# Transposing K as fp32 pairs and multiplying V two rows at a time in a decode attention kernel

## The chip, the cores and the metric

The kernel runs on one core of one Trainium2 chip. The metric is device time in microseconds (us) of that core. Every number below is from fast runs. The queue that issues DMA transfers is SP's; PE is the TensorE matmul engine, PEld its weight loads (counted apart, they overlap PE: busy 1139 and 817 us in a span of 1375 in before), DVE the VectorE, ACT the ScalarE, POOL the GpSimd. "GB/s" is what the core's 16 DMA engines moved.

## The reference, cut to what matters

```
x (1,1,448); k_cache, v_cache (1, 8, 65536, 256) bf16; 16 query heads, 2 per K/V head
q = x @ wq                                   # 16 heads of 256
s = q . k / sqrt(256);  p = softmax(s);  o = p . v
a = o @ wo
b = (relu-gated FFN of a second x: 448 -> 1792 -> 448)
g = sigmoid(sum(x * gate_w));  out = g * a + (1 - g) * b
```

K and V are 268 MB each and every byte is used once. The arithmetic per byte is small (PE is busy 1139 and DVE 1006 of 1375 us in before), so the limit taken here is the time in which 549 MB (with the weights) can be read: 1286 us at the 427 GB/s of the stretch where only V arrives.

## The kernel before

The K rows of a head come in 16 groups of 4096 rows (2 MB), 32 rows to a partition. A group goes one of two ways. A **T group** goes to PE: transpose K, evict by ACT, multiply by q (QK). A **D group** goes to DVE, which multiplies and sums each row with a broadcast q. The constant `ND_PER_HEAD` says how many of the 16 are D groups: 6 and 5 in turn. A V group goes to PE (PV). The loads go into three rings of 2 MB slots: three for T, two for D, three for V.

```python
def emit_tp(slot, blk, c, bank):              # T: 8 rows x one half of the head dim
    kb = KTp[bank][:].bitcast(BF16)
    for jj in range(8):
        j = blk * 8 + jj
        transpose(out=kb[:, jj*128:(jj+1)*128], in_=tring[:, slot, j, c*128:(c+1)*128], identity=ident)

def emit_qk(g, sl0, kbufs, sphys, ...):       # 2 slots x 2 halves, 512 columns each
    for sp_ in range(2):
        for c in range(2):
            matmul(S_ps[sphys], lhsT=zq[:, g, c, 63-r:191-r], rhs=kts[:, kbufs[c], sp_*512:(sp_+1)*512])

def emit_pv(g, grp, slot, j0, j1, ...):       # one row of V for each matmul
    for j in range(j0, j1):
        matmul(O_ps[qd:qd+2, 0:256], lhsT=lhs, rhs=vring[:, slot, j, :])
...
```

All loads are issued from one in-order queue, SP's. Their order is fixed when the program is built: a small scheduler in the builder keeps estimated costs (`D_TP`, `D_QK`, `D_V`, ...) and picks at each moment the load whose engine will run dry first. On the chip, SP waits for the slot of the next load in that order, even if another ring has a free slot: by the author's count from the trace of after, about 24 us of its loss fell where SP waited for a T slot while a V slot stood free. The FFN weights are loaded at the end into the memory of the K ring.

```python
cands.append((pri, c, g, grp, slot))     # for c in "TDV", if its next slot is free
...
cands.sort()                             # the least work ahead of its engine goes first; T before V
...
dma_q.append((..., emit_wdma(key, dst, src, ring_keys_for(e0, e1)), ..., k_all_consumed))   # FFN weights
```

## Time and profile before

The time before is 1374.0 us (median of 15 runs, 1369.6 to 1379.5).

| | before |
|---|---|
| bytes read | 549 MB |
| rate while only V arrives (1300 to 1320 us) | 424 GB/s; 424 to 429 in the windows around it |
| PE, DVE, ACT busy | 1139, 1006, 413 us |
| T group on PE | 7.03 us |
| D group on DVE | 22.1 us (64 products, 346 ns apart) |
| one 2 MB transfer at 427 GB/s | 4.9 us |

The head of the page of before, busy time and share of the span, with the DMA queues (packets, MB, share of 16 engines' span):

```profile
span 1375.1 us, 30278 instructions
...
PE 1138.9 (83%) x11218; PEld 816.5 (59%) x11218; DVE 1006.4 (73%) x5706; ACT 413.0 (30%) x834; POOL 12.9 (1%) x29
...
q1 hardware_dynamic: 45186, 549.05, 96.2%
q8 instruction: 87, 1.43, 0.4%
q14 instruction: 62, 0.51, 0.1%
```

Data alone hold the 16 DMA engines 96% of the span, and no compute engine is near that.

Windows of 20 us of before: the stretch, its length, then busy us of PE, PEld, DVE, ACT and POOL with their instructions in brackets, then granted PE clock, DMA share, GB/s:

```profile
0.00:20.00 20.00, 1.46 (x22) 1.35 (x23) 0.00 (x0) 0.00 (x0) 5.43 (x12) 1.00 0.82 269
200.00:220.00 20.00, 20.00 (x210) 14.33 (x208) 12.45 (x67) 8.21 (x16) 0.00 (x0) 0.97 0.71 286
540.00:560.00 20.00, 20.00 (x235) 14.80 (x234) 20.00 (x117) 12.02 (x23) 0.00 (x0) 1.00 0.90 366
1160.00:1180.00 20.00, 7.96 (x112) 7.05 (x112) 0.42 (x3) 0.00 (x0) 0.00 (x0) 0.59 0.70 248
1300.00:1320.00 20.00, 15.06 (x134) 10.86 (x133) 0.00 (x0) 0.00 (x0) 0.00 (x0) 1.00 1.00 424
```

The last line is the undisturbed stream. The others show where it falls short: the start, stretches in which PE is busy all the time, and the FFN weights. At 427 GB/s, 549 MB take 1286 us, so 1374 - 1286 = 88 us are lost somewhere.

The chain of waits of before, in a stretch of T groups alone (start us, us, what):

```profile
97.34 1.79 PE KTp L427 x32
99.13 0.86 PE S_ps L441 x4
99.99 0.45 PE KTp L427 x8
100.44 0.86 PE S_ps L441 x4
101.30 1.34 PE KTp L427 x24
102.64 1.73 PE S_ps L441 x8
```

From one block of 32 transposes to the next (97.34 to 104.37) 7.03 us pass: 64 transposes at 56 ns and 16 QK matmuls at 216 ns.

What the SP queue of before waited for (us in total, times, longest):

```profile
SPq L137 <- PE O_ps L571: 521.6, 93, 20.7
SPq L137 <- PE KTp L427: 472.3, 59, 31.4
SPq L137 <- DVE S_T L458: 210.9, 31, 18.7
```

SP nearly always waits for a slot, as a loader that is faster than its rings must. Most of this waiting cost nothing: these waits sum to 1205 us, the loss to 88.

### The profile page before, as it was taken

To read this page: it belongs to the slowest core of one execution; us is meant where nothing else is said; L and a number is where in the kernel's file an instruction comes from. 1 tells how busy PE (TensorE), PEld (TensorE's weight loads), DVE (VectorE), ACT (ScalarE), POOL (GpSimd) and SP (SyncE) were. 2 spreads that over 40 slices of the span, in tenths; PEclk is the share of its full clock that TensorE was granted. 3 is DMA by queue.
4 is the path that set the end of the run, shared out by engine and by line. 5 is a ranking of instruction groups with operands and counts; after the bars stand their busy time and mean duration, and the time that the engine had idled before them with its cause. 6 is when DMAs were issued, how large, how long until landed. Compare 5 with 4: busy or idle time off the path is not lost.

```text
span 1375.1 us, 30278 instructions
## 1 busy us (share of the span) xinstructions
PE 1138.9 (83%) x11218; PEld 816.5 (59%) x11218; DVE 1006.4 (73%) x5706; ACT 413.0 (30%) x834; POOL 12.9 (1%) x29
## 2 busy tenths in 40 slices
PE   4899989896899767996779897898778987687776
PEld 3577657674666545764457565576556755455554
DVE  1999997989997999799998972799939993000000
ACT  1466535440344202730026410463014620010000
POOL 1000000000000000000000000000000000000000
PEclk9999999998899978998899999999999999799999
DMA  8999998999999999999998999999999997999996
GB/s 335 397 406 413 422 426 347 413 394 430 383 405 403 417 393 377 410 426 404 420 430 352 417 398 428 410 426 413 419 419 400 417 389 317 372 427 428 426 428 292
DMA packets 45335, 550.98 MB, mean 401 GB/s; under 512 B 5185, under 2 KB 11074, under 8 KB 11970
## 3 DMA queue, kind: packets, MB, share of 16 engines
q1 hardware_dynamic: 45186, 549.05, 96.2%
q8 instruction: 87, 1.43, 0.4%
q14 instruction: 62, 0.51, 0.1%
HBM read 549.03 MB, written 0.00 MB: 399 GB/s over the span
## 4 chain that ended last, share of the span: by engine, by line
DMA 38%; PE 35%; DVE 24%; ACT 1%; issue 1%; SPq 1%; ACTq 0%; DVEq 0%
DMA vraw<-in_A_v_cache_dram 26%; DVE junk L458 23%; PE KTp L427 12%; PE O_ps L571 11%; PE S_ps L441 11%; DMA kring<-in_A_k_cache_dram 10%; DMA kring<-in_B_W_gate_dram 1%; DMA vraw<-in_A_wq_dram 1%; PE M_ps L385 1%; DMA kring<-in_B_W_up_dram 1%; DVE S_T L458 1%; ACT P_sb L503 1%; ACT kts L432 0%; SPq L371 0%; DVE MXW L472 0%
## 5 line engine op out<-in xcount | busy, mean ns | idle before, releaser
L458 DVE CUSTOM_DVE_ANT_0 junk<-kring,qb 128x256 bf16<-128x256 bf16 x2816 | 976.1, 421 | 1.4 <-DMA kring<-in_A_k_cache_dram 0.8
L432 ACT COPY kts<-KTp 128x512 f32<-128x512 f32 x672 | 355.9, 595 | 412.6 <-PE KTp L427 412.3
L571 PE MATMUL O_ps<-vraw,PT_sb 128*2 128x256 bf16 x2688 | 324.6, 282 | 101.9 <-DMA vraw<-in_A_v_cache_dram 101.4
L427 PEld LDWEIGHTS KTp<-ident,kring 128*128 128x128 bf16 x5376 | 330.1, 100 | 100.5 <-DMA kring<-in_A_k_cache_dram 39.5
L427 PE MATMUL KTp<-ident,kring 128*128 128x128 bf16 x5376 | 353.9, 223 | 35.3 <-DMA kring<-in_A_k_cache_dram 34.4
L571 PEld LDWEIGHTS O_ps<-vraw,PT_sb 128*2 128x2 bf16 x2688 | 229.4, 88 | 194.9 <-DMA vraw<-in_A_v_cache_dram 119.1
L441 PE MATMUL S_ps<-kts,zq 128*128 128x512 bf16 x1344 | 336.2, 382 | 1.1 <-ACT kts L432 1.1
L458 DVE DVE_READ_ACCUMULATOR2_ANT S_T<- 128x1 f32 x2816 | 235.3, 84 | 0.0
L571 PE MATMUL O_ps<-vraw,PTd 128*2 128x256 bf16 x1408 | 173.4, 285 | 62.4 <-DMA vraw<-in_A_v_cache_dram 62.4
L571 PEld LDWEIGHTS O_ps<-vraw,PTd 128*2 128x2 bf16 x1408 | 120.2, 87 | 114.8 <-DMA vraw<-in_A_v_cache_dram 72.3
L441 PEld LDWEIGHTS S_ps<-kts,zq 128*128 128x128 bf16 x1344 | 121.0, 98 | 103.1 <-ACT kts L432 15.9
L578 ACT COPY o_raw<-O_ps 2x256 f32<-2x256 f32 x8 | 2.9, 363 | 426.6 <-PE O_ps L571 426.6
L643 DVE SCALAR_TENSOR_TENSOR res_bf<-A_ps,gsc,res 1x448 bf16<-1x448 f32 x1 | 0.7, 671 | 154.2 <-PE A_ps L609 154.2
L543 DVE TENSOR_REDUCE den<-den 128x2 f32<-128x6 f32 x8 | 1.3, 159 | 100.7 <-POOL den L536 100.7
L472 DVE TENSOR_REDUCE MXW<-S_sb 64x1 f32<-64x512 f32 (+2 forms) x32 | 21.7, 677 | 40.6 <-ACT S_sb L448 40.1
L385 PE MATMUL M_ps<-xT,vraw 128*128 128x1 bf16 (+1 forms) x128 | 9.2, 174 | 18.5 <-DMA vraw<-in_A_wq_dram 18.5
L503 ACT ACTIVATE P_sb<-S_sb,nbias 64x512 bf16<-64x512 f32 (+2 forms) x32 | 23.0, 718 | 0.6
L496 ACT ACTIVATE nbias<-negm 128x2 f32<-128x2 f32 x8 | 1.7, 209 | 69.3 <-DVE negm L494 69.2
L400 DVE CAST zq<-M_ps 128x32 bf16<-128x32 f32 x1 | 0.3, 297 | 28.0 <-PE M_ps L392 28.0
L385 PEld LDWEIGHTS M_ps<-xT,vraw 128*128 128x128 bf16 (+1 forms) x128 | 8.3, 106 | 19.4 <-issue 18.5
L625 DVE TENSOR_SCALAR g_bf<-M_ps 128x14 bf16<-128x14 f32 x1 | 0.2, 173 | 22.2 <-PE M_ps L619 22.2
L619 PE MATMUL M_ps<-xT,kring 128*128 128x1 bf16 x112 | 8.0, 173 | 8.0 <-DMA kring<-in_B_W_up_dram 4.9
(47 smaller groups left out, 102.1 us busy)
## 6 DMA issues: line engine op xcount, KB each, us to landing
kring<-in_A_k_cache_dram SPq DMA_DIRECT2D x128, 2048.0 KB, 12.2
vraw<-in_A_v_cache_dram SPq DMA_DIRECT2D x128, 2048.0 KB, 11.6
wo_sb<-in_A_wo_dram SPq DMA_DIRECT2D x1, 3584.0 KB, 46.6
vraw<-in_A_wq_dram SPq DMA_DIRECT2D x1, 3072.0 KB, 13.3
kring<-in_B_W_down_dram SPq DMA_DIRECT2D x1, 1568.0 KB, 8.2
kring<-in_B_W_gate_dram SPq DMA_DIRECT2D x1, 1344.0 KB, 13.7
kring<-in_B_W_up_dram SPq DMA_DIRECT2D x1, 1344.0 KB, 5.6
vraw<-in_A_wq_dram SPq DMA_DIRECT2D x1, 512.0 KB, 14.8
```

Of the source, the lines that this page charges most:

```text
L385: A("pe", (lambda hc=hc, kt=kt, kk=kk: lambda e: e.matmul(M_ps[:, MC_Q + hc:MC_Q + hc + 1], lhsT=wq_sb[0:kk, kt, hc * 128:(hc + 1) * 128], ...
L427: A("pe", (lambda j=j, jj=jj: lambda e: e.transpose(out=kb[:, jj * 128:(jj + 1) * 128], in_=tring[:, slot, j, c * 128:(c + 1) * 128], iden ...
L432: A("act", lambda e: e.copy(out=kts[:, kbuf, :].bitcast(F32), in_=KTp[bank][:, :]), pr=PQ(B_K + bank), w=[("kts", kbuf)], tag=f"ev b{bank} ...
L441: A("pe", (lambda r=r, c=c, sp_=sp_, first=first, last=last: lambda e: e.matmul(S_ps[sphys][:, :], lhsT=zq[:, g, c, 63 - r:191 - r], rhs=k ...
L458: A("dve", (lambda j=j, hh=hh, col=col, ji=ji: lambda e: e.tensor_tensor_reduce(out=junk[:, ji, :], in0=dring[:, slot, j, :], in1=qb[:, g, ...
L472: A("dve", (lambda hh=hh, p0=p0: lambda e: e.tensor_reduce(out=MXW[p0:p0 + ns, pb, 2 + 2 * b + hh:3 + 2 * b + hh], in_=S_sb[p0:p0 + ns, pb ...
L496: A("act", lambda e: e.activation(out=nbias[:, pb, :], in_=negm[:, pb, :], func=ACT.Copy, scale=SCALE), r=[("negm", pb)], w=[("nbias", pb) ...
L503: A("act", lambda e: e.activation(out=P_sb[p0:p0 + ns, pb, b, :], in_=S_sb[p0:p0 + ns, pb, b, :], func=ACT.Exp, bias=nbias[p0:p0 + ns, pb, ...
L543: A("dve", lambda e: e.tensor_reduce(out=den[:, pb, :], in_=src, axis=AX.X, op=AluOpType.add), r=[("den6", pb)], w=[("den", pb)], tag=f"de ...
L571: A("pe", (lambda lhs=lhs, j=j, f_=f_, l_=l_: lambda e: e.matmul(O_ps[qd:qd + 2, 0:DH], lhsT=lhs, rhs=vring[:, slot, j, :], start=f_, stop ...
L578: A("act", lambda e: e.copy(out=o_raw[qd:qd + 2, :], in_=O_ps[qd:qd + 2, 0:DH]), pr=PQ(B_O, qd, qd + 2), w=[("oraw", pb)], tag=f"oc g{g}")
L619: A("pe", (lambda ft=ft, kt=kt, kk=kk: lambda e: e.matmul(M_ps[:, col0 + ft:col0 + ft + 1], lhsT=w_sb[0:kk, kt, ft * 128:(ft + 1) * 128], ...
```

## The change

Two bf16 neighbours are taken as one fp32, so that one transpose moves a whole row of 256 values per partition: 32 transposes in a T group instead of 64. After it, even and odd elements lie interleaved, so QK reads its moving operand with stride 2, and q is prepared in the same order. PV takes two rows at once: 4 weight columns (2 rows x 2 heads) against 512 columns of V; half of the products are not wanted and are not used. Head sums then come from two places, which doubles the small matmuls at the end of a head. `ND_PER_HEAD` becomes (6, 6): four T groups become D groups. The intent is less PE work and half the PE instructions.

```diff
-    ND_PER_HEAD=(6, 5),
+    ND_PER_HEAD=(6, 6),
...
-        def emit_tp(slot, blk, c, bank):
-            kb = KTp[bank][:].bitcast(BF16)
-            for jj in range(8):
-                    out=kb[:, jj * 128:(jj + 1) * 128], in_=tring[:, slot, j, c * 128:(c + 1) * 128], identity=ident[:]))(),
+        def emit_tp(slot, blk, bank):
+            for jj in range(4):
+                    out=KTp[bank][:, jj * 128:(jj + 1) * 128], in_=tring[:, slot, j, :].bitcast(F32), identity=identf[:]))(),
...
+            for par in range(2):
+                rhs = kts[:, kbuf, :].rearrange("p (n e) -> p e n", e=2)[:, par, :]
...
-                    O_ps[qd:qd + 2, 0:DH], lhsT=lhs, rhs=vring[:, slot, j, :], start=f_, stop=l_))(),
+                rhs = vring[:, slot, j:j + 2, :].rearrange("p a d -> p (a d)")
+                    O_ps[qd:qd + 4, 0:2 * DH], lhsT=lhs, rhs=rhs, start=f_, stop=l_))(),
...
-        D_TP, D_QK, D_EV = 0.46, 0.88, 0.52
-        D_V = J * 0.11
+        D_TP, D_QK, D_EV = 0.45, 0.46, 0.60
+        D_V = (J // 2) * 0.225
```

Cut: the same regrouping in the builder's scheduler, the q projection, and the tail of each head.

More of the change, by code (lines that the diff above doesn't have):

```diff
@@ L219, in bass_gated_mix__gqa_block_cached__glu_gated_reglu__decode_kernel @@
     GROWS = 128 * J
-    assert SK % GROWS == 0 and J % 8 == 0
+    assert SK % GROWS == 0 and J % 4 == 0
     NG = SK // GROWS
-    NBLK = J // 8
-    SLOTS_PER_GROUP = 2 * NBLK
+    NBLK = J // 4
+    SLOTS_PER_GROUP = NBLK
     ndc = CFG["ND_PER_HEAD"]
@@ L307, in bass_gated_mix__gqa_block_cached__glu_gated_reglu__decode_kernel @@
         rden = sb("rden", [128, HKV, 2], F32)
-        o_raw = sb("o_raw", [64, DH], F32)
-        oT = sb("oT", [128, 2, 4], BF16)
-        res = sb("res", [1, D], F32)
+        o_raw = sb("o_raw", [64, 2 * DH], F32)
+        oT = sb("oT", [128, 2, 8], BF16)
+        res = junk[0:1, :, :].rearrange("p a d -> p (a d)").bitcast(F32)[:, 0:D]
         res_bf = sb("res_bf", [1, D], BF16)
@@ L382, in emit_qproj @@
             for hc in range(NHC):
+                h_, e_ = divmod(hc, 2)
                 for kt in range(KT):
                     kk = ksz[kt]
-                    A("pe", (lambda hc=hc, kt=kt, kk=kk: lambda e: e.matmul(
-                        M_ps[:, MC_Q + hc:MC_Q + hc + 1], lhsT=wq_sb[0:kk, kt, hc * 128:(hc + 1) * 128],
+                    wv = wq_sb[0:kk, kt, h_ * DH:(h_ + 1) * DH].rearrange("p (n e) -> p e n", e=2)[:, e_, :]
+                    A("pe", (lambda hc=hc, kt=kt, kk=kk, wv=wv: lambda e: e.matmul(
+                        M_ps[:, MC_Q + hc:MC_Q + hc + 1], lhsT=wv,
                         rhs=xT[0:kk, kt:kt + 1], start=(kt == 0), stop=(kt == KT - 1)))(),
@@ L419, in emit_qb_ev @@
         def emit_qb_ev(g, bank):
-            A("act", lambda e: e.activation(out=qb[:, g, :, :].rearrange("p h d -> p (h d)"), in_=KTp[bank][:, :], func=ACT.Copy),
+            dst = qb[:, g, :, :].rearrange("p h (n e) -> p h e n", e=2)
+            src = KTp[bank][:, :].rearrange("p (h e n) -> p h e n", h=2, e=2)
+            A("act", lambda e: e.activation(out=dst, in_=src, func=ACT.Copy),
               pr=PQ(B_K + bank), w=[("qb", g)], tag=f"qbev{g}")
-        def emit_tp(slot, blk, c, bank):
-            kb = KTp[bank][:].bitcast(BF16)
-            for jj in range(8):
-                j = blk * 8 + jj
+        def emit_tp(slot, blk, bank):
+            for jj in range(4):
+                j = blk * 4 + jj
                 A("pe", (lambda j=j, jj=jj: lambda e: e.transpose(
-                    out=kb[:, jj * 128:(jj + 1) * 128], in_=tring[:, slot, j, c * 128:(c + 1) * 128], identity=ident[:]))(),
-                  r=[("T", slot), "ident"], pw=PQ(B_K + bank), tag=f"tp s{slot} b{blk} c{c}")
+                    out=KTp[bank][:, jj * 128:(jj + 1) * 128], in_=tring[:, slot, j, :].bitcast(F32), identity=identf[:]))(),
+                  r=[("T", slot), "identf"], pw=PQ(B_K + bank), tag=f"tp s{slot} b{blk}")
         def emit_ev(bank, kbuf):
@@ L433, in emit_ev, with emit_qk @@
               pr=PQ(B_K + bank), w=[("kts", kbuf)], tag=f"ev b{bank}->k{kbuf}")
-        def emit_qk(g, sl0, kbufs, sphys, first_of_bank, last_of_bank):
-            for sp_ in range(2):
-                r = (sl0 + sp_) % 64
-                for c in range(NC2):
-                    first = first_of_bank and sp_ == 0 and c == 0
-                    last = last_of_bank and sp_ == 1 and c == NC2 - 1
-                    A("pe", (lambda r=r, c=c, sp_=sp_, first=first, last=last: lambda e: e.matmul(
-                        S_ps[sphys][:, :], lhsT=zq[:, g, c, 63 - r:191 - r], rhs=kts[:, kbufs[c], sp_ * 512:(sp_ + 1) * 512],
-                        start=first, stop=last))(),
-                      r=[("kts", kbufs[c]), "zq"], pw=PQ(B_S + sphys), tag=f"qk g{g} sl{sl0 + sp_}")
+        def emit_qk(g, sl, kbuf, sphys, first_of_bank, last_of_bank):
+            r = sl % 64
+            for par in range(2):
+                first = first_of_bank and par == 0
+                last = last_of_bank and par == 1
+                rhs = kts[:, kbuf, :].rearrange("p (n e) -> p e n", e=2)[:, par, :]
+                A("pe", (lambda r=r, par=par, rhs=rhs, first=first, last=last: lambda e: e.matmul(
+                    S_ps[sphys][:, :], lhsT=zq[:, g, par, 63 - r:191 - r], rhs=rhs, start=first, stop=last))(),
+                  r=[("kts", kbuf), "zq"], pw=PQ(B_S + sphys), tag=f"qk g{g} sl{sl}")
         def emit_scopy(g, b, sphys):
@@ L548, in slot_of @@
         def slot_of(g, ti, j):
-            blk, rem = divmod(j, 8)
-            sp_, q4 = divmod(rem, 4)
-            sl = ti * SLOTS_PER_GROUP + blk * 2 + sp_
+            blk, q4 = divmod(j, 4)
+            sl = ti * SLOTS_PER_GROUP + blk
             return sl // 64, sl % 64, q4
@@ L558, in emit_pv @@
             idx = PATHS[g][:grp].count(path)
-            for j in range(j0, j1):
+            assert j0 % 2 == 0 and j1 % 2 == 0
+            for j in range(j0, j1, 2):
                 if path == "T":
                     b, r, q4 = slot_of(g, idx, j)
+                    assert q4 % 2 == 0
                     base = (b * 4 + q4) * 128
-                    lhs = PT_sb[:, pb, base:base + 128].rearrange("p (h r) -> p r h", h=2)[:, r, :]
+                    lhs = PT_sb[:, pb, base:base + 256].rearrange("p (h r) -> p r h", h=4)[:, r, :]
                     rk = [("PT", pb)]
@@ L566, in emit_pv @@
                     col = (idx * J + j) * 2
-                    lhs = PTd[:, pb, col:col + 2]
+                    lhs = PTd[:, pb, col:col + 4]
                     rk = [("PTd", pb, 0), ("PTd", pb, 1)]
                 f_ = first and j == j0
-                l_ = last and j == j1 - 1
-                A("pe", (lambda lhs=lhs, j=j, f_=f_, l_=l_: lambda e: e.matmul(
-                    O_ps[qd:qd + 2, 0:DH], lhsT=lhs, rhs=vring[:, slot, j, :], start=f_, stop=l_))(),
-                  r=[("V", slot)] + rk, pw=PQ(B_O, qd, qd + 2), tag=f"pv g{g} grp{grp}")
+                l_ = last and j == j1 - 2
+                rhs = vring[:, slot, j:j + 2, :].rearrange("p a d -> p (a d)")
+                A("pe", (lambda lhs=lhs, rhs=rhs, f_=f_, l_=l_: lambda e: e.matmul(
+                    O_ps[qd:qd + 4, 0:2 * DH], lhsT=lhs, rhs=rhs, start=f_, stop=l_))(),
+                  r=[("V", slot)] + rk, pw=PQ(B_O, qd, qd + 4), tag=f"pv g{g} grp{grp}")
         def emit_oc(g):
@@ L577, in emit_oc @@
             qd = 32 * pb
-            A("act", lambda e: e.copy(out=o_raw[qd:qd + 2, :], in_=O_ps[qd:qd + 2, 0:DH]),
-              pr=PQ(B_O, qd, qd + 2), w=[("oraw", pb)], tag=f"oc g{g}")
+            A("act", lambda e: e.copy(out=o_raw[qd:qd + 4, :], in_=O_ps[qd:qd + 4, 0:2 * DH]),
+              pr=PQ(B_O, qd, qd + 4), w=[("oraw", pb)], tag=f"oc g{g}")
         def emit_ft(g):
@@ L583, in emit_ft @@
             qd = 32 * pb
-            for c in range(NC2):
-                col = MC_OT + pb * 4 + c * 2
-                A("pe", (lambda c=c, col=col: lambda e: e.transpose(
-                    out=M_ps[:, col:col + 2], in_=o_raw[qd:qd + 2, c * 128:(c + 1) * 128],
-                    identity=identf[qd:qd + 2, qd:qd + 2]))(),
+            for i in range(4):
+                col = MC_OT + pb * 16 + i * 4
+                A("pe", (lambda i=i, col=col: lambda e: e.transpose(
+                    out=M_ps[:, col:col + 4], in_=o_raw[qd:qd + 4, i * 128:(i + 1) * 128],
+                    identity=identf[qd:qd + 4, qd:qd + 4]))(),
                   r=[("oraw", pb), "identf"], pw=PQ(B_M), tag=f"ft g{g}")
@@ L592, in emit_on @@
             pb = g % 2
-            for hh in range(2):
-                src = M_ps[:, MC_OT + pb * 4:MC_OT + pb * 4 + 4].rearrange("p (c h) -> p h c", h=2)[:, hh, :]
-                dst = oT[:, pb, :].rearrange("p (c h) -> p h c", h=2)[:, hh, :]
-                A("act", (lambda hh=hh, src=src, dst=dst: lambda e: e.activation(
-                    out=dst, in_=src, func=ACT.Copy, scale=rden[:, g, hh:hh + 1]))(),
-                  r=[("rden", g)], pr=PQ(B_M), w=[("oT", pb, hh)], tag=f"on g{g}")
+            for part in range(2):
+                for hh in range(2):
+                    c0 = MC_OT + pb * 16 + part * 8 + 2 * part + hh
+                    src = M_ps[:, c0:c0 + 8].rearrange("p (c k) -> p c k", k=4)[:, :, 0]
+                    dst = oT[:, pb, part * 4:part * 4 + 4].rearrange("p (c h) -> p h c", h=2)[:, hh, :]
+                    A("act", (lambda src=src, dst=dst, hh=hh: lambda e: e.activation(
+                        out=dst, in_=src, func=ACT.Copy, scale=rden[:, g, hh:hh + 1]))(),
+                      r=[("rden", g)], pr=PQ(B_M), w=[("oT", pb, part, hh)], tag=f"on g{g}")
         def emit_am(g):
@@ L602, in emit_am @@
             n = 0
-            for c in range(NC2):
-                for hh in range(2):
-                    n += 1
-                    first = (g == 0 and n == 1)
-                    last = (g == HKV - 1 and n == 2 * NC2)
-                    hc = (2 * g + hh) * NC2 + c
-                    A("pe", (lambda c=c, hh=hh, hc=hc, first=first, last=last: lambda e: e.matmul(
-                        A_ps[0:1, 0:D], lhsT=oT[:, pb, 2 * c + hh:2 * c + hh + 1], rhs=wo_sb[:, hc, :],
-                        start=first, stop=last))(),
-                      r=[("oT", pb, 0), ("oT", pb, 1), "wo"], pw=PQ(B_A, 0, 1), tag=f"am g{g}")
+            for part in range(2):
+                for c in range(NC2):
+                    for hh in range(2):
+                        n += 1
+                        first = (g == 0 and n == 1)
+                        last = (g == HKV - 1 and n == 4 * NC2)
+                        hc = (2 * g + hh) * NC2 + c
+                        oc_ = part * 4 + c * 2 + hh
+                        A("pe", (lambda oc_=oc_, hc=hc, first=first, last=last: lambda e: e.matmul(
+                            A_ps[0:1, 0:D], lhsT=oT[:, pb, oc_:oc_ + 1], rhs=wo_sb[:, hc, :],
+                            start=first, stop=last))(),
+                          r=[("oT", pb, a_, b_) for a_ in range(2) for b_ in range(2)] + ["wo"], pw=PQ(B_A, 0, 1),
+                          tag=f"am g{g}")
         def emit_gu(which):
@@ L641, in emit_final @@
             A("dve", lambda e: e.tensor_scalar(out=res[:], in0=b_sb[:], scalar1=gsc[0:1, 3:4], scalar2=None, op0=AluOpType.mult),
-              r=[("gsc", 3), "b_sb"], w=["res"], tag="fin0")
+              r=[("gsc", 3), "b_sb"], w=["res"] + [("junk", i) for i in range(4)], tag="fin0")
             A("dve", lambda e: e.scalar_tensor_tensor(out=res_bf[:], in0=A_ps[0:1, 0:D], scalar=gsc[0:1, 2:3], in1=res[:],
@@ L702, in pe_work_ahead @@
             w = max(0.0, S.busy["pe"] - S.now)
-            w += sum(NBLK * (2 * D_TP + D_QK) for _ in arrived["T"])
+            w += sum(NBLK * (D_TP + D_QK) for _ in arrived["T"])
             w += sum(D_V for _ in arrived["V"])
@@ L738, in pick_dma @@
                 if c == "V":
-                    work = pe_work_ahead() + inflight["T"] * NBLK * (2 * D_TP + D_QK) + inflight["V"] * D_V
+                    work = pe_work_ahead() + inflight["T"] * NBLK * (D_TP + D_QK) + inflight["V"] * D_V
                     kleft = NG - k_done[g] - (0 if g == 0 else 0)
@@ L742, in pick_dma @@
                 elif c == "T":
-                    work = pe_work_ahead() + inflight["T"] * NBLK * (2 * D_TP + D_QK) + inflight["V"] * D_V
+                    work = pe_work_ahead() + inflight["T"] * NBLK * (D_TP + D_QK) + inflight["V"] * D_V
                     pri = work
@@ L779, in s_bank_for @@
             first = cur["filled"] == 0
-            cur["filled"] += 2
+            cur["filled"] += 1
             last = cur["filled"] == cur["total"]
@@ L784, in pick_pe @@
         def pick_pe():
-            if pend_qk and pend_qk[0]["ev"] == 2:
+            if pend_qk and pend_qk[0]["ev"] == 1:
                 blk = pend_qk[0]
@@ L792, in start @@
                     def start(blk=blk, phys=phys, first=first, last=last):
-                        emit_qk(blk["g"], blk["sl0"], blk["kbufs"], phys, first, last)
+                        emit_qk(blk["g"], blk["sl0"], blk["kbuf"], phys, first, last)
                     def done(blk=blk, phys=phys, last=last, cur=cur):
-                        for c in range(2):
-                            kts_free[blk["kbufs"][c]] = True
+                        kts_free[blk["kbuf"]] = True
                         g = blk["g"]
@@ L828, in pick_pe @@
                 bank = ktp_rr[0] % 3
-                can_t = ktp_free[bank] and len(pend_qk) <= 2
+                can_t = ktp_free[bank] and len(pend_qk) <= 3
             can_v = False
@@ L850, in pick_pe, with start, done @@
                 ktp_free[bank] = False
-                sub = tc["sub"]
-                blk, c = divmod(sub, 2)
+                blk = tc["sub"]
                 tc["sub"] += 1
-                lastsub = tc["sub"] == 2 * NBLK
+                lastsub = tc["sub"] == NBLK
                 info = dict(tc)
-                def start(info=info, blk=blk, c=c, bank=bank):
-                    emit_tp(info["slot"], blk, c, bank)
-                def done(info=info, blk=blk, c=c, bank=bank, lastsub=lastsub):
-                    if c == 0:
-                        sl0 = info["ti"] * SLOTS_PER_GROUP + blk * 2
-                        pend_qk.append(dict(g=info["g"], sl0=sl0, kbufs={}, ev=0, lastblk=(blk == NBLK - 1)))
-                    qkb = [q for q in pend_qk if q["g"] == info["g"] and q["sl0"] == info["ti"] * SLOTS_PER_GROUP + blk * 2][0]
-                    pend_ev.append((bank, qkb, c))
+                def start(info=info, blk=blk, bank=bank):
+                    emit_tp(info["slot"], blk, bank)
+                def done(info=info, blk=blk, bank=bank, lastsub=lastsub):
+                    sl0 = info["ti"] * SLOTS_PER_GROUP + blk
+                    qkb = dict(g=info["g"], sl0=sl0, kbuf=None, ev=0, lastblk=(blk == NBLK - 1))
+                    pend_qk.append(qkb)
+                    pend_ev.append((bank, qkb))
                     if lastsub:
@@ L893, in pick_act @@
         def pick_act():
-            for i, (bank, qkb, c) in enumerate(pend_ev):
+            for i, (bank, qkb) in enumerate(pend_ev):
                 kb = kts_rr[0] % 4
@@ L902, in start, with done @@
                         emit_ev(bank, kb)
-                    def done(bank=bank, kb=kb, qkb=qkb, c=c):
+                    def done(bank=bank, kb=kb, qkb=qkb):
                         ktp_free[bank] = True
-                        qkb["kbufs"][c] = kb
+                        qkb["kbuf"] = kb
                         qkb["ev"] += 1
@@ L1026, in am_done @@
                                 try_final()
-                        pe_q.append((0.8, lambda: emit_am(g), am_done))
+                        pe_q.append((1.6, lambda: emit_am(g), am_done))
                     def queue_on():
                         if chain[g].get("rden"):
-                            act_q.append((0.5, lambda: emit_on(g), on_done))
+                            act_q.append((0.9, lambda: emit_on(g), on_done))
                         else:
@@ L1034, in ft_done @@
                     queue_on()
-                pe_q.append((0.25, lambda: emit_ft(g), ft_done))
+                pe_q.append((0.5, lambda: emit_ft(g), ft_done))
             act_q.append((0.3, lambda: emit_oc(g), oc_done))
```

## The prediction

> **What bounds the kernel now.** The DMA. The queue table counts 549 MB; in the last 150 us, where only V arrives, the 20 us windows show 424 to 429 GB/s. 549 MB at 427 GB/s is 1286 us of the 1375 us span, so at most about 85 us (6%) can be won. In the windows, about 30 us of that is fixed: the start (269 GB/s in the first 20 us), the FFN weights, which wait for all K (346 and 248 GB/s from 1140 to 1180 us), and the end. The other 55 us lie where rings are full: 286 GB/s at 200-220, 369 at 280-300, 358 at 360-380, 366 at 540-560, 329 at 720-740 us, with PE busy 20.0 of 20 us in most. The SP queue's waits name PV (522 us), transposes (472) and DVE (211): an in-order queue blocked on a slot. So PE bursts, not PE's average, cost time.
>
> **Costs per 2 MB group (a DMA needs 4.9 us).** From the chain of waits and the timeline, unthrottled:
> - T group: 64 bf16 transposes, 56 ns each, 3.58 us, + 16 QK matmuls, 216 ns each, 3.46 us = 7.03 us.
> - V group: 32 PV matmuls, 3.54 us.
> - D group on DVE: 64 x 346 ns = 22.1 us.
>
> Per head (157 us of DMA) PE has 10.5 T + 16 V = 130 us and DVE about 125 us.
>
> **What the change does.**
> 1. fp32-pair transposes: 64 become 32 per T group. No fp32 128x128 transpose is in the trace. The small fp32 transposes have 135 ns weight loads against 99 to 107 for bf16. [...] I estimate 112 ns each, two bf16 ones: no gain. Outer cases: 56 ns (T group 5.3 us) or 224 ns (10.6 us).
> 2. QK stays 16 matmuls of 512 columns; the moving operand now has stride 2. Estimate 216 to 230 ns. ACT evictions stay 8 a group at 595 ns.
> 3. PV: 16 matmuls of 512 columns, 16 x 216 = 3.46 us; saves only 0.1 us a group, 10 us of PE in total, although instructions halve.
> 4. ND_PER_HEAD (6,6): 4 groups go from T to D: PE and ACT lose 28 and 19 us, DVE gains 88 us (1006 to 1095).
> 5. Tail: double the scalings and output matmuls per head, 1 to 2 us exposed once.
>
> **On the critical path.** PE per head falls from 130 to about 126 us, DVE rises to about 137; both stay under 157. DVE idled about 110 us before the K phase ended at 1144, mostly at 800-880 and 1000-1040, where K had run ahead, so most of the extra DVE work fills idle time; K ends later (1160 to 1210), with still enough V behind it to fill the DMA. I expect 10 to 20 us of the burst losses back; the replanned queue order may give or take some.
>
> **Prediction.** 1360 us, 80% range 1325 to 1395. Faster by over 2% 0.27, within 2% 0.60, slower by over 2% 0.13.
>
> **What would show it.** Transposes 112 ns apart in runs; QK pitch 216 to 230; PV pitch 216; PE busy down but not halved; DVE busy near 1095; V-only tail still at 427 GB/s; fewer 20 us windows under 380 GB/s.
>
> **What would make it wrong.** Transposes at 224 ns: PE total near 1300 us, PE-bound, 1400 or more. At 56 ns: bursts vanish, 1330 or less. DVE becoming the limit: K ending after 1260. Strided QK reads slower than 260 ns. A worse replanned order with new head-of-line blocking.

1375 us less the 10 to 20 us expected back, itself an estimate, comes to 1355 to 1365, and 1360 is the middle. The 112 ns stand as the estimate, twice the 56 ns of a bf16 transpose in the trace of before; the outer cases are once and four times the 56 ns. The 1 to 2 us of the tail are an estimate too.

## The result, and the profile after

Ratios here and below are the mean time of one kernel's fast runs over the mean of the kernel before's fast runs of the same rounds, so not quite the ratio of the medians quoted beside them.

After: 1372.5 us (median of 12 runs, 1368.2 to 1377.9); before 1374.0. The ratio is 0.9992, with a 95% interval of 0.9975 to 1.0009. The change is worth nothing that these runs can see.

The same lines of the page of after:

```profile
span 1371.7 us, 20995 instructions
...
PE 1130.8 (82%) x6338; PEld 618.8 (45%) x6338; DVE 1095.0 (80%) x6218; ACT 411.2 (30%) x818; POOL 13.6 (1%) x29
...
q1 hardware_dynamic: 45186, 549.05, 96.4%
q8 instruction: 49, 0.80, 0.2%
q14 instruction: 65, 0.53, 0.1%
```

PE has little more than half of its instructions left, yet is busy as long as before. DVE has gained 89 us.

Windows of after:

```profile
0.00:20.00 20.00, 3.79 (x55) 3.45 (x55) 0.00 (x0) 0.00 (x0) 5.43 (x12) 1.00 0.82 288
180.00:200.00 20.00, 19.24 (x108) 9.63 (x107) 19.95 (x117) 9.01 (x21) 0.66 (x1) 1.00 0.86 337
540.00:560.00 20.00, 20.00 (x135) 13.89 (x134) 20.00 (x117) 12.34 (x24) 0.00 (x0) 1.00 0.95 381
1180.00:1200.00 20.00, 13.06 (x107) 7.01 (x104) 0.48 (x3) 6.24 (x19) 0.46 (x1) 0.87 0.56 204
1300.00:1320.00 20.00, 14.83 (x67) 5.31 (x66) 0.00 (x0) 0.00 (x0) 0.00 (x0) 1.00 1.00 426
```

The V-only rate is the same, and so are the kinds of window that fall short. The chain in a stretch of T groups alone, after:

```profile
121.46 1.31 PE KTp L430 x12
122.77 0.45 PE S_ps L444 x2
123.22 0.44 PE KTp L430 x4
123.66 1.36 PE S_ps L444 x6
```

This is half a T group (16 transposes, 8 matmuls); the next one begins at 125.02, 3.56 us later. The whole takes 7.11 us: 32 transposes 109 ns apart and 16 matmuls 226 ns apart. Waits of SP after:

```profile
SPq L137 <- PE O_ps L575: 522.2, 95, 17.1
SPq L137 <- PE KTp L430: 423.6, 59, 31.4
SPq L137 <- DVE S_T L460: 256.2, 36, 19.9
```

The sizes, from the starts of the instructions in the traces (medians; the matmuls of PV in runs):

| | before | after |
|---|---|---|
| one transpose | 56 ns | 109 ns |
| one QK matmul | 216 ns | 226 to 227 ns |
| T group, pace in a run of them | 7.03 us | 7.11 us |
| PV in a run, per 32 rows | 32 x 109 ns = 3.49 us | 16 x 216 ns = 3.46 us |
| T, D groups in all | 84, 44 | 80, 48 |
| last DVE product ends at | 1151 us | 1179 us |

Here an fp32 transpose of 128 columns takes almost exactly as long as two bf16 ones (109 ns against 2 x 56), and a PV matmul of 512 columns as long as two of 256 (216 ns against 2 x 109). All that is left of the intended gain is the move of four T groups, 28 us of PE work (less the 80 x 0.08 = 6 us by which the remaining T groups became slower). So the question is why that moved nothing, when the prediction gave it 10 to 20 us.

### The profile page after: what moved, and what is told of

Same layout as the page of the kernel before. It is cut to its first block, busy times and chain, and to the rows that moved or that the text cites. A ratio compares the mean times of both kernels' runs of the same rounds, so it can differ in the third digit from the quotient of the medians.

```text
span 1371.7 us, 20995 instructions
## 1 busy us (share of the span) xinstructions
PE 1130.8 (82%) x6338; PEld 618.8 (45%) x6338; DVE 1095.0 (80%) x6218; ACT 411.2 (30%) x818; POOL 13.6 (1%) x29
## 4 chain that ended last, share of the span: by engine, by line
PE 40%; DMA 32%; DVE 24%; ACT 2%; issue 1%; SPq 1%; POOL 0%; ACTq 0%; POOLq 0%; DVEq 0%
DVE junk L460 22%; DMA vraw<-in_A_v_cache_dram 19%; PE KTp L430 14%; PE S_ps L444 14%; PE O_ps L575 11%; DMA kring<-in_A_k_cache_dram 10%; DMA kring<-in_B_W_gate_dram 1%; DMA vraw<-in_A_wq_dram 1%; DMA kring<-in_B_W_up_dram 1%; DVE MXW L474 1%; PE M_ps L387 1%; DVE S_T L460 1%; ACT kts L435 1%; ACT P_sb L505 1%; SPq L371 0%
## 5 line engine op out<-in xcount | busy, mean ns | idle before, releaser
L460 DVE CUSTOM_DVE_ANT_0 junk<-kring,qb 128x256 bf16<-128x256 bf16 x3072 | 1064.9, 422 | 0.6 <-ACT qb L424 0.2
L575 PE MATMUL O_ps<-vraw,PT_sb 128*4 128x512 bf16 x1280 | 310.3, 399 | 97.2 <-DMA vraw<-in_A_v_cache_dram 97.1
L430 PE MATMUL KTp<-identf,kring 128*128 128x128 f32 x2560 | 348.4, 278 | 32.3 <-DMA kring<-in_A_k_cache_dram 32.3
L430 PEld LDWEIGHTS KTp<-identf,kring 128*128 128x128 f32 x2560 | 308.0, 144 | 115.7 <-DMA kring<-in_A_k_cache_dram 37.7
L460 DVE DVE_READ_ACCUMULATOR2_ANT S_T<- 128x1 f32 x3072 | 259.7, 85 | 0.0
L575 PE MATMUL O_ps<-vraw,PTd 128*4 128x512 bf16 x768 | 193.3, 410 | 72.3 <-DMA vraw<-in_A_v_cache_dram 72.3
L575 PEld LDWEIGHTS O_ps<-vraw,PT_sb 128*4 128x4 bf16 x1280 | 110.0, 90 | 287.9 <-DMA vraw<-in_A_v_cache_dram 120.7
L575 PEld LDWEIGHTS O_ps<-vraw,PTd 128*4 128x4 bf16 x768 | 65.6, 90 | 196.3 <-DMA vraw<-in_A_v_cache_dram 89.3
L474 DVE TENSOR_REDUCE MXW<-S_sb 64x1 f32<-64x512 f32 (+1 forms) x32 | 21.7, 678 | 44.8 <-ACT S_sb L450 44.3
L505 ACT ACTIVATE P_sb<-S_sb,nbias 64x512 bf16<-64x512 f32 (+1 forms) x32 | 23.0, 717 | 0.6
## 6 DMA issues: line engine op xcount, KB each, us to landing
vraw<-in_A_wq_dram SPq DMA_DIRECT2D x1, 512.0 KB, 12.5
```

What stands on the lines that cost most here:

```text
L430: A("pe", (lambda j=j, jj=jj: lambda e: e.transpose(out=KTp[bank][:, jj * 128:(jj + 1) * 128], in_=tring[:, slot, j, :].bitcast(F32), iden ...
L460: A("dve", (lambda j=j, hh=hh, col=col, ji=ji: lambda e: e.tensor_tensor_reduce(out=junk[:, ji, :], in0=dring[:, slot, j, :], in1=qb[:, g, ...
L474: A("dve", (lambda hh=hh, p0=p0: lambda e: e.tensor_reduce(out=MXW[p0:p0 + ns, pb, 2 + 2 * b + hh:3 + 2 * b + hh], in_=S_sb[p0:p0 + ns, pb ...
L505: A("act", lambda e: e.activation(out=P_sb[p0:p0 + ns, pb, b, :], in_=S_sb[p0:p0 + ns, pb, b, :], func=ACT.Exp, bias=nbias[p0:p0 + ns, pb, ...
L575: A("pe", (lambda lhs=lhs, rhs=rhs, f_=f_, l_=l_: lambda e: e.matmul(O_ps[qd:qd + 4, 0:2 * DH], lhsT=lhs, rhs=rhs, start=f_, stop=l_))(), ...
```

## The experiments

The candidate theories were: (A) the cost of a T group on PE sets the loss in the stretches where PE is saturated, and the change leaves that cost alone; (B) the parts gain and lose and cancel; (C) the one in-order queue blocks on a full ring; (D) the rings are too coarse; (E), formed last, the DMA itself is held back by something the kernel does. All the kernels passed the comparison with the reference. A saturated window is one in which PE is busy 19.5 of 20 us or more. Unless said otherwise a run has three timed rounds.

| run | what | median us | ratio to before, 95% interval |
|---|---|---|---|
| after | the change | 1372.5 | 0.9992 (0.9975 to 1.0009) |
| nd_only | before, ND (6,6) | 1370.0 | 0.9986 (0.9963 to 1.0009) |
| code_only | after, ND (6,5) | 1366.9 | 0.9959 (0.9936 to 0.9983) |
| pv_only | before + batched PV | 1371.4 | 0.9982 (0.9952 to 1.0012) |
| tp_only | before + fp32 transposes | 1372.3 | 1.0007 (0.9967 to 1.0046) |
| half_qk | after, half of QK | 1367.2 | 0.9959 (0.9944 to 0.9975) |
| even_order | after, T and V interleaved | 1365.9 | 0.9955 (0.9940 to 0.9971) |
| ffn_free | after, FFN loads unchained | 1365.5 | 0.9942 (0.9925 to 0.9959) |
| order_and_ffn | both of these | 1361.0 | 0.9914 (0.9890 to 0.9938) |
| even_before | before + both of these | 1363.0 | 0.9926 (0.9905 to 0.9947) |
| v_own_queue | after, V loads from POOL | 1419.5 | 1.0350 (1.0334 to 1.0365) |
| d_own_queue | order_and_ffn, D loads from POOL | 1356.7 | 0.9892 (0.9876 to 0.9909) |
| d_own_65 | the same, ND (6,5) | 1355.7 | 0.9880 (0.9856 to 0.9905) |
| fine_after | after, 1 MB groups | 1384.1 | 1.0077 (1.0036 to 1.0118) |
| fine_before | before, 1 MB groups | 1383.4 | 1.0075 (1.0041 to 1.0108) |
| fine_free | fine_after, FFN unchained | 1375.0 | 1.0016 (0.9995 to 1.0036) |
| fine_even | fine_after, both | 1373.0 | 0.9999 (0.9978 to 1.0019) |
| fine_even_before | fine_before, both | 1368.2 | 0.9960 (0.9933 to 0.9988) |
| dve_fetch | fine_even, more DVE instructions | 1423.5 | 1.0365 (1.0340 to 1.0390) |

### The parts alone

nd_only is before with `-ND_PER_HEAD=(6, 5)` / `+ND_PER_HEAD=(6, 6)`. code_only is after with the same line undone. pv_only takes from the change `emit_pv`, the tail of a head and `D_V`; tp_only takes the rest without `ND_PER_HEAD`.

> The kernel before, with ND_PER_HEAD (6,6) alone. Theory A (the change leaves what fills the DMA alone: a T group takes PE about 7.1 us in T-only stretches whatever the share of D, and the fixed losses stay): ratio to before 0.995 to 1.003, DVE busy near 1095 us, PE T groups 80, so 28 us less PE work that buys nothing. Theory B (the parts gain and lose and cancel): moving 4 groups off PE gains, ratio 0.985 to 0.992, about 15 us.

> The kernel after with ND_PER_HEAD back at (6,5): both code changes, no shift of groups. Theory A: ratio 0.997 to 1.005, T group 7.1 us, V group 3.5 us. Theory B: the code changes lose what the shift gains, ratio 1.008 to 1.015.

> The kernel before with the batched PV alone (bf16 transposes, ND (6,5)). Theory A: PV pitch near 219 ns for 512 columns against 2 x 111, ratio 0.996 to 1.003. Theory B: batching gains by itself, ratio 0.985 to 0.992.

> The kernel before with the fp32-pair transposes and the strided QK alone (single-row PV, ND (6,5)). Theory A: transposes about 109 ns, QK 226 ns, T group 7.1 us against 7.03; ratio 0.998 to 1.005. Theory B: the stride-2 QK costs 10 ns x 1344 = 13 us on the critical path, ratio 1.006 to 1.015.

Three of the four intervals contain 1. code_only is 0.4% ahead of before, not behind it, which theory B had needed it to be; why it is ahead stays unexplained (each of these kernels also has its own load order, since the builder plans it anew). tp_only paces its T groups at 7.11 us with transposes 109 ns apart, and does not lose. So nothing large is being cancelled: no part is worth more than about half a percent. nd_only is the sharper half of the answer: 28 us of PE work moved away bought 0.14%, within noise.

### Is PE's cost of a T group what the saturated stretches cost?

```diff
-            for par in range(2):
+            for par in range(1):
```

This leaves out half of each score (it passed the comparison all the same, so that comparison says little of the scores). Its output is wrong, which doesn't matter for the time. The order of everything stayed.

> The kernel after with only one of the two QK matmuls per block, the order of everything as it was; the result is wrong on purpose. A T group then costs PE about 5.3 us in place of 7.1. Theory A (in T-only stretches PE's cost of a T group sets the DMA rate, about 390 GB/s and less): the saturated stretches shrink and with them most of their 27 us of loss; 1340 to 1355 us, ratio 0.975 to 0.988. Rival (the DMA loses time for other reasons: the in-order queue, mixed streams, DVE): PE becomes idler and the time stays, ratio 0.995 to 1.003.

Windows of half_qk:

```profile
540.00:560.00 20.00, 18.89 (x129) 13.20 (x127) 20.00 (x117) 14.04 (x27) 0.00 (x0) 1.00 0.97 385
620.00:640.00 20.00, 13.08 (x56) 4.56 (x53) 20.00 (x117) 0.00 (x0) 0.00 (x0) 0.93 0.88 358
680.00:700.00 20.00, 14.36 (x84) 10.18 (x83) 20.00 (x117) 6.89 (x13) 0.00 (x0) 0.83 0.85 346
1180.00:1200.00 20.00, 12.30 (x124) 8.04 (x124) 0.33 (x2) 5.74 (x18) 0.46 (x1) 0.79 0.43 137
```

The pace of a T group fell to 6.1 us, not to the 5.3 expected: ACT's evictions now stand in PE's way (1.17 us for two, between PE's pieces), as the chain of waits of half_qk shows:

```profile
98.02 1.17 ACT kts L435 x2
99.19 0.05 issue
99.24 0.40 PE S_ps L444
99.64 1.31 PE KTp L430 x12
```

Still, the saturated windows are all but gone (2 in place of 18): in them, after had lost 27 us against 427 GB/s and half_qk loses 1.6. The time fell by 0.3% against after, about 5 us. The loss turned up in windows where PE is not saturated: between 40 and 1140 us these had lost 22 us in after and lose 42 in half_qk. Theory A fell: PE's saturation marks where the loss is seen, but taking it away leaves most of the loss, in other windows.

### The order of the loads and the FFN weights

In the order that the builder makes, T loads come in runs of up to a head, then V loads in runs. even_order replaces the choice between T and V by one rule, here and in the same way where PE's next work is picked:

```diff
+                    drop = "T" if pt - pv > 1.5 else "V"      # K ahead of V by 1.5 heads at most
+                    cands = [c for c in cands if c[1] != drop]
```

ffn_free removes a false order. The five FFN weight loads named the same ring slots as written, so each waited for the one before it, though they write disjoint ranges:

```diff
-            return A("sp", ..., w=[key] + list(extra_w), ...)
+            deps = [...]           # shortened: last writer and readers of each ring slot beneath
+            return A("sp", ..., w=[key], after=deps, ...)
```

> The kernel after with T and V transfers interleaved evenly (K ahead of V by 1.5 heads at most) in place of runs of T followed by runs of V; the same instructions in another order. Theory A: fewer PE-saturated windows with a low DMA rate, 15 to 30 us gained, ratio 0.978 to 0.990. Rival (the losses do not come from the runs of T): ratio 0.996 to 1.004.

> The kernel after without the false order among the five FFN weight loads (each waited for the one before, as all name the same ring slots, though they write disjoint ranges). Prediction: of the 14 us lost in the two windows after K has ended, 6 to 10 us come back, ratio 0.992 to 0.996. If the loss is the wait for the end of K itself: ratio 0.998 to 1.002.

> Even order and free FFN loads together. If both losses are separate, the gains add: 1335 to 1350 us, ratio 0.972 to 0.984. If one takes over the other's gain, no better than the better of the two alone.

> The kernel before with even order and free FFN loads: the counterpart of order_and_ffn (1361 us, ratio 0.991). If the change is worth nothing in this order too: ratio 0.988 to 0.995. If the runs of T had hidden a gain of the change (less PE work, fewer T groups), this one is 0.5% or more behind order_and_ffn: ratio over 0.996.

The FFN's false order cost 0.5% (0.9942 against 0.9992 of after, 7 us): as expected. The even order gave 0.4%, a third of the least that was expected, and the two together 0.8%, half of the least expected. The change is still worth nothing in the better order: even_before 0.9926, order_and_ffn 0.9914, with intervals that overlap almost wholly.

### A queue of its own for one ring

From the trace of after, each wait of SP was put beside the time at which every slot had come free. By the author's count, 24 of the 83 us lost against 427 GB/s fell where SP waited for a T slot while a V slot stood free. So the V loads were moved to POOL's queue, and in another kernel, on top of order_and_ffn, the D loads:

```diff
-            A("sp", lambda e: e.dma_start(dst, src), w=[(cls, slot)],
+            A("pool" if cls == "V" else "sp", lambda e: e.dma_start(dst, src), w=[(cls, slot)],     # v_own_queue
+            A("pool" if cls == "D" else "sp", ...                                                   # d_own_queue
```

> The kernel after with the V loads issued from POOL's queue; K and weights stay on SP's. Nothing else changes. Worked out from the trace of after (wait of the SP queue for each slot, the time at which each slot had come free, and bytes moved in each us): of 83 us lost against 427 GB/s, about 24 us fall where SP waited for a T slot while a V slot stood free, 7 where it waited for V while a T slot stood free. Theory C (the in-order queue, blocked on a full ring while another ring has a free slot): 15 to 30 us gained, ratio 0.978 to 0.990. Rival (rings are simply too short, or the DMA slows in mixed streams): ratio 0.996 to 1.004. A third outcome, that loads from POOL cost more by themselves, would show as a V-only tail under 424 GB/s.

> The kernel with even order and free FFN loads, and the D loads on POOL's queue. There SP waits 703 us for DVE's slots, mostly with T or V slots free. Theory C: 10 to 25 us better than order_and_ffn, 1336 to 1351 us, ratio 0.973 to 0.984. Rival: as order_and_ffn, ratio 0.989 to 0.994.

v_own_queue became 3.5% slower. Its V-only tail still reached 429 GB/s (1300 to 1320 us; 405 and 412 in the next two windows), so a load from POOL need not be slow by itself. But there are stretches at 258 GB/s (420 to 440 us) and 307 GB/s (600 to 620 us), in which DVE was busy only 11.3 and 9.3 of 20 us: V loads ran ahead while D loads were late. That V took their bandwidth is argued from these windows, not shown. d_own_queue gained 4 us on order_and_ffn by the medians, where 10 to 25 were expected, and the intervals overlap. So blocking of the queue is worth little at most, and freeing it can do harm: theory C fell. That the harm comes from the order, which is also what shares out the bandwidth, is argued.

### Finer rings

```diff
-    J=32, NT=3, ND=2, NV=3, ND_PER_HEAD=(6, 6)
+    J=16, NT=6, ND=4, NV=6, ND_PER_HEAD=(12, 12)
```

> The kernel after with groups of 1 MB in place of 2 MB and twice the slots (T 6, D 4, V 6; 12 D groups of 32 a head): the same memory, the same bytes, the same matmuls. Found in the trace of after: most of the dips in the DMA rate begin where only one or two transfers are in flight, because a slot of 2 MB comes free late and all at once. Theory D (ring granularity sets the loss): slots come free twice as often, more transfers are in flight, 20 to 40 us gained, ratio 0.970 to 0.987. Rival (the order of the one in-order queue sets it, whatever the slot's size): ratio 0.995 to 1.003. If 1 MB transfers are worse by themselves, the V-only tail falls under 424 GB/s.

> The kernel before with the same finer rings (12 and 10 D groups of 32 a head). Theory D: ratio to before 0.970 to 0.987 too, and fine_after within 0.5% of it, the change still worth nothing. If PE's cost had been hidden behind the rings, fine_after would now be 1% or more better than fine_before.

> The kernel after with 1 MB groups and free FFN loads, in the old order. Against fine_even it tells what the order is worth with fine rings: if the order matters, 10 to 20 us slower than fine_even, ratio 0.988 to 0.997; if the rings' fineness alone had mended it, the same as fine_even.

> The kernel after with 1 MB groups, even order and free FFN loads. Worked out from fine_after: its V-only tail runs at 421 GB/s, so 549 MB take 1304 us; the FFN stretch lost about 19 us there and the rest of the middle about 33. If both go: 1335 to 1350 us, ratio 0.972 to 0.983. If only the FFN stretch is mended: ratio 0.990 to 0.997.

> The kernel before with the same three edits. If the change is worth nothing once the DMA is nearly always fed: within 0.4% of fine_even. If it is worth its 27 us less PE work there: 1% or more behind fine_even.

Theory D fell too: 0.8% slower. One reason is plain: with 1 MB transfers the V-only tail runs at 419 to 424 GB/s, 1.5% under the tail of 2 MB ones. The other reason opened the last question. fine_even was expected at 1335 to 1350 us and took 1373; fine_free, in the old order, took 1375, so with fine rings the order is worth nothing that shows. In before and after, one or two transfers are in flight for about half of the time. In fine_even ten or eleven are, from 680 us to the end of K, and still the DMA does not run at its rate. Windows of fine_even:

```profile
440.00:640.00 200.00, 162.23 (x867) 84.63 (x880) 184.22 (x1053) 61.97 (x127) 1.86 (x4) 0.97 1.01 420
700.00:1100.00 400.00, 325.56 (x1739) 170.86 (x1768) 375.75 (x2139) 121.83 (x245) 2.72 (x6) 0.97 1.00 406
1280.00:1340.00 60.00, 46.68 (x208) 15.44 (x205) 0.00 (x0) 1.30 (x5) 0.00 (x0) 1.00 1.01 422
```

For the change: fine_after and fine_before came in at 1.0077 and 1.0075 in the same rounds. In fine_even against fine_even_before, also of the same rounds, the changed code is 0.4% behind: its runs took 1371.7 to 1374.2 us, the others 1365.4 to 1370.0. With the DMA fed as well as it can be here, the 28 us less PE work buy nothing, and the change costs about 5 us (its q14 has 69 packets in place of 65).

### One landing of sixteen behind the other fifteen

The traces hold sixteen landing records for every transfer (in after 432 for the 27 transfers into the first T slot), as many as the page counts DMA engines. They are read here as one of each engine; the records do not name it. Sorted, as us after the first of the sixteen, and averaged over the transfers of a stretch:

```
                          1st   8th   14th  15th  16th
after      800-1000 us    0.0   0.4   1.1   1.5    2.8
fine_even  100- 200 us    0.0   1.0   2.0   2.2    6.3
fine_even  500- 600 us    0.0   1.1   2.3   2.4   16.6
fine_even  800-1000 us    0.0   0.5   1.3   1.9   20.1
fine_even 1250-1340 us    0.0   0.5   1.0   1.7    3.2
```

In fine_even fifteen landings come within 2.4 us on average, and one falls ever further behind, to 20 us. Meanwhile the stream goes from 420 GB/s (440 to 640 us) to 406 (700 to 1100 us), against 422 in the tail. The author's reading: one engine lags, nearly all the slots come to wait for it, and from then on the whole stream has its pace. In the V-only tail, when DVE is idle, the lag is down to 3.2 us. (That the late landing is of the same engine each time is inferred from the steady growth of the lag.) In after, with one or two transfers in flight for about half of the time, the lag is 2.8 us; that each pause of the stream lets the engine catch up is the author's reading too.

What holds it back? The two queues that the page calls "instruction" (q8 and q14; a packet of theirs is called a fetch here) carry little, but the author's guess was that all the fetches of one of them fall to one engine. q8 goes with PE: its packets fall from 87 to 49 with the change (1.43 to 0.80 MB), as the instructions of PE and PEld fall from 22436 to 12676. It is not the suspect, for the rate from 700 to 1100 us is 405 GB/s of data in fine_even and 406 in fine_even_before, and q8 goes on in the tail (5 of its 49 packets in after start behind DVE's last product). q14 all but stops when DVE stops (2 of 65 packets there). So DVE was given more instructions that do no work:

```diff
+            if eng_name == "dve" and (op.tag or "").startswith("ttr"):
+                for _ in range(3):
+                    eng.wait_ge(sems["pool"], 1)          # satisfied long before
             ins = op.fn(eng)
```

> fine_even with three waits on an already satisfied semaphore before each DVE product: 9216 instructions more on DVE, which do no work. In fine_even 10 to 11 transfers are in flight from 700 to 1100 us, yet the DMA moves 405 GB/s of its 421: of the 16 completions of a transfer, one comes about 18 us after the other fifteen, always one alone. Theory E (the DMA engine that also fetches DVE's instructions, queue q14, 0.43 GB/s there, is that one): [...]the rate in such a stretch falls to 385 to 395 GB/s, and the time rises 15 to 35 us above fine_even (1388 to 1408 us). Rival (something else holds that engine back): rate 403 to 407, time 1368 to 1378 us. If DVE itself is slowed by the waits (products more than 350 ns apart), the run tells nothing.

The queue q14 of fine_even, then of dve_fetch, from their pages:

```profile
q14 instruction: 69, 0.56, 0.1%
```

```profile
q14 instruction: 115, 0.94, 0.2%
```

Windows of dve_fetch, in the same stretches as above:

```profile
440.00:640.00 200.00, 161.52 (x847) 86.07 (x848) 181.48 (x1033) 57.14 (x112) 1.40 (x3) 0.95 0.99 400
700.00:1100.00 400.00, 314.76 (x1671) 160.97 (x1672) 356.42 (x2022) 110.40 (x220) 1.83 (x4) 0.97 0.98 388
```

DVE's products stayed 346 ns apart, so DVE was not slowed. q14 rose by 46 packets with 9216 instructions more on DVE, so it is taken as the queue of DVE's instructions. Its bytes rose by 0.38 MB, 0.07% of the data (a larger rise had been expected), and the kernel took 50 us longer, by the medians: about 1 us for each packet more. The rate from 700 to 1100 us fell from 406 to 388 GB/s, within the 385 to 395 that was expected; the time was expected to rise by 15 to 35 us, and rose by more. The lag of the sixteenth landing is 21.5 us there. That DVE's instruction stream slows the stream of data is thus shown by adding to it; taking some away was not tried. That it does so through one engine is inferred, from the one late landing.

How strong is it? An estimate from these rates, if the sixteen engines share the data evenly and the slowest, which serves all the fetches, sets the pace: per engine, the undisturbed stream of 1 MB groups is 421/16 = 26.3 GB/s. With 0.43 GB/s of DVE fetches (700 to 1100 us, fine_even) the slowest engine is down by (421 - 405)/16 = 1.0 GB/s of data; with 0.74 GB/s (dve_fetch) by (421 - 387)/16 = 2.1. So each fetched byte would displace 2.4 to 2.9 bytes of data on that engine (from the unrounded rates).

The traces also show the delay fetch by fetch, for 2 MB transfers too. In the V-only tail the last landing of one K or V transfer and that of the next are 4.89 us apart (2.48 for 1 MB). What exceeds this was summed, from 57 us (when the first weights are in) to DVE's last product, over all pairs of neighbours, and over those between whose last landings a q14 packet starts:

| run | pairs | excess, us | pairs with a q14 fetch | their excess, us | by chance, us |
|---|---|---|---|---|---|
| before | 211 | 59.5 | 53 | 22.8 | 18 |
| after | 217 | 55.9 | 55 | 39.8 | 17 |
| half_qk | 217 | 51.4 | 56 | 45.4 | 16 |
| order_and_ffn | 217 | 53.4 | 55 | 46.4 | 16 |
| fine_even | 433 | 48.3 | 61 | 42.3 | 9 |
| dve_fetch | 433 | 96.9 | 104 | 77.3 | 30 |

"By chance" is the mean of "their excess" when all the fetch times are shifted together against the landings, 500 times. The median excess of a pair with a fetch is 0.95 to 0.97 us in the last four rows, 0.94 in after and 0.38 in before, and 0.00 without one in all six. So in after some 40 of these 56 us come with DVE's fetches, and some 16 lie in the other pairs. half_qk took 10 of these 16 away, but the pairs with a fetch became 6 us longer in all: the sum fell by 4.5 us, the time by about 5. From before to after it is alike: the other pairs lose 16 us in place of 37, the pairs with a fetch 40 in place of 23, and the sum hardly moves. A reading that fits, from one trace of each kernel and not tested: where the stream pauses for another reason, the lagging engine catches up and its fetch costs nothing, so that mending the pause lays the fetch bare. In before the fetches do not stand out from chance, and what the 37 us are made of stays open.

### A version that beats both

> A candidate for a version that beats both: d_own_queue with ND_PER_HEAD (6,5), since code_only (6,5) stood 0.3% ahead of after (6,6). If the gains add: 1350 to 1356 us, ratio 0.983 to 0.989. If not: as d_own_queue, 0.988 to 0.992.

d_own_65 (the changed code with ND (6,5), even order, free FFN loads, D loads on POOL's queue) took 1355.7 us, 1.2% under before, the best of all the runs. It is not measurably ahead of d_own_queue. In it, too, the sixteenth landing lies 13 us behind the first on average from 400 to 1000 us. This is within the 2% that count as the same here, though the interval excludes 1. Its counterpart with the code of before was not run; as the change gained nothing in the other pairs, the gain is most likely the loader's.

## Why the prediction was wrong

- **"What bounds the kernel now. The DMA."** Right. The V-only tail stayed at 424 to 429 GB/s, and no compute engine's cost decided the time; what it left out is that the DMA is slower while DVE runs (406 GB/s against 422 with DVE idle, in fine_even).
- **Costs of the parts.** Right for the paces: transposes 112 ns estimated, 109 measured; QK 216 to 230 estimated, 226 measured; PV 216 at 512 columns, measured 216; DVE 1095 us, measured 1095.0; end of K at 1160 to 1210 us, measured 1179 (DVE's last product). The busy sums were not: PE was to lose 28 us by the moved groups and 10 by PV and lost 8, ACT was to lose 19 and lost 2. No speed-up came from fp32 transposes, as said. The estimate was twice the bf16 pace, and 109 ns against 56 is what the traces show; why it is so, no run shows.
- **"at most about 85 us (6%) can be won ... The other 55 us lie where rings are full".** Misplaced. The ceiling of 427 GB/s was taken from a stretch in which DVE is idle. While DVE runs, a well fed stream has 406 of 421 GB/s (fine_even, 1 MB groups), and dve_fetch, with 46 more packets of DVE's instructions, 388. In after, with 2 MB groups, 40 of the 56 us that the stream lost while DVE worked lie in the pairs with a DVE fetch. So most of what the prediction booked on full rings and PE's bursts is, in after, not theirs. (The sum itself is loose: 1375 - 1286 is 89 us, not 85.)
- **"So PE bursts, not PE's average, cost time" and "I expect 10 to 20 us of the burst losses back".** This is the step that failed: that less waiting behind PE comes back as time. First, the change does not shorten a burst: within one, a T group takes 7.11 us instead of 7.03; only the number of T groups falls, by 4 of 84, and nd_only shows that this buys nothing measurable. Second, half_qk did shorten the T group, by 14%, and emptied the saturated windows (27 us of loss became 1.6), yet gained only 5 us, as the other windows lost 20 us more. The windows with PE at 20.0 of 20 us showed where the shortfall became visible, not what caused it. What took the place of the PE bursts, in after, is the delay that comes with each of DVE's fetches, by about 0.95 us each (put down to the one lagging engine): outside the pairs with a fetch the excess did fall, from 37 to 16 us, but in these pairs it rose from 23 to 40. The change also adds D groups, and with them q14 packets (62 before, 65 after).
- **"the replanned queue order may give or take some".** Right as a caution: the order is worth about 5 us and the FFN's false order about 7, more than anything in the change.

The forecast of 1360 us was 12.5 us low. The measured time lay in its wide range and in the likeliest class (within 2%), which a forecast of no gain would have met as well; the gain of 1% it foresaw is not there. Fewer windows under 380 GB/s came about, as forecast (8 in place of 12), and bought nothing.

What stays open: how the loss of before divides between DVE's fetches and the rings; which DMA engine lands late, and whether it is always the same; whether fewer DVE instructions for the same work would win time, as only adding some was tried; why code_only is ahead; and why moving the V loads to POOL's queue cost 47 us.

## What to carry to other kernels

Halving the number of instructions on an engine buys nothing when each of the remaining ones takes twice as long (transposes of 109 ns for 56), and work taken off an engine that is not the limit bought next to nothing either (28 us of PE in nd_only: 0.14%, within noise): look for the pace (start to start) and for the stage's limit, not for busy time. A saturated engine beside a starving DMA may be a coincidence until that engine's cost has been cut and the time has followed. And take the roofline from a stretch in which all the engines run as they do in the rest of the kernel: the stream's rate with DVE idle was 4% too high here (422 against 406 GB/s, in fine_even).
